# Two more weight slices loaded in column halves on two DMA queues, beside ScalarE's first table load

## The chip, the cores and the metric

One core of a Trainium2 chip. The metric is the device time of one execution in microseconds (us), of the slowest (here the only) core. In a profile, PE is TensorE's matmul stream, PEld its weight loads, DVE VectorE, ACT ScalarE, POOL GpSimd, SP SyncE; SPq and ACTq are the queues on which SyncE and ScalarE issue DMA loads. The "table load" is ACT_TABLE_LOAD, which in the trace stands on ScalarE just before its first activation (1.28 us, from 1.18 us on, in the kernel before).

## The reference

```python
def _fwd_reference(x, w1, w2):                 # x (1, 2048, 640), w1 (640, 1536), w2 (1536, 640), bf16
    h = jnp.einsum("bsd,df->bsf", x, w1)
    h = jax.nn.silu(h)
    return jnp.einsum("bsf,fd->bsd", h, w2)

def reference(x, w1, w2, grad_out):
    out, vjp = jax.vjp(_fwd_reference, x, w1, w2)
    return (out, *vjp(grad_out))               # out, and the gradients of x, w1, w2
```

## The kernel before

The change lies in the first 10 us. The kernel's first stage computes h for the first 512 rows of x. w1 lies in SBUF (the core's own memory, to which the loads go) as five row slices of 128 rows (k = 0 to 4, 384 KB each). The stage takes them in turn: for each slice twelve matmuls of 128x256, each pair of them accumulating into one of six tiles of PSUM (the memory to which matmuls write). So slice k has to be complete before its last matmuls, and slice k+1 is wanted 12 matmuls later.

```python
        def load_w1(k, cols=slice(0, F), eng=nc.sync):
            return eng.dma_start(out=w1_nat[:, k, cols], in_=w1_v[:, k, cols])

        early += [load_x(nc.sync, 0), load_x(nc.scalar, 1)]
        early += [load_w1(0, slice(0, F // 2)), load_w1(0, slice(F // 2, F), nc.scalar)]
        early += [load_w1(k) for k in range(1, 3)]
        for k in range(3, DT):
            load_w1(k)
        nc.sync.dma_start_transpose(out=xT_next[:, :, HC:SC], in_=x2[HC:SC, :])
        start_before_entry_wait(nc, {i.ins.name for i in early})   # moved ahead of the program's entry barrier
        nc.scalar.activation(warm_a[:], warm[:, 0:1], ACT.Silu)    # brings the first table load
        nc.sync.dma_start(out=w2_nat[:], in_=w2_v[:])
        goT_next = load_goT(0)
        # ... w2T and w1T by DMA transpose ...

        def h_first(xT, aT, ghT):
            pe_x(xT)                     # PE transposes of the two early x tiles
            # ...
            for dt_ in range(DT):        # slice by slice
                for pair in range(NPAIR):
                    h_pair_mm(hs[0][pair], pair, dt_, xT, halves[0])   # two matmuls
            # ... then the second 256 rows of x, with all slices present ...
```

The program's framework orders the instructions of each engine itself and gives each DMA one of eight completion semaphores. A DMA that takes over a semaphore waits until the DMA that had it before has landed: in the trace of this kernel the first eight loads have eight different semaphores, and the ninth DMA, the transpose of x's second half, is issued at 3.09, when the second x tile, whose semaphore it takes over, has landed (3.08).

## Time and profile before

| | before |
|---|---|
| time, median of 3 runs before the prediction | 320.84 us (320.25 to 321.2) |
| span of the profiled run | 318.8 us |
| PE busy | 313.6 us, 98% |
| first h stage: PE's idle time put down to w1 loads | 0.22 + 0.65 us |

Two lines of the profile's page, kernel before: the busy table (busy us, share of the span, count of instructions) and the chain of work that ended last, by engine.

```profile
PE 313.6 (98%) x1516; PEld 150.5 (47%) x1544; DVE 102.8 (32%) x182; ACT 76.8 (24%) x139; POOL 0.7 (0%) x6
...
PE 96%; DMA 2%; issue 1%; SPq 0%; DVE 0%; DVEq 0%
```

TensorE bounds the kernel. A change of loads can gain only what PE idles for them.

From the timeline of the first 20 us, kernel before (a selection of its lines): start in us, length in us, engine, source line, operation, output<-inputs, count, and in brackets how long the engine was idle and what ended that. w1's tile and tensor show as `w_nat` and `in_w_dram`.

```profile
0.09 0.39 SPq L183 DMA_DIRECT2D x_nat<-in_x_dram  x1
0.21 0.38 ACTq L183 DMA_DIRECT2D x_nat<-in_x_dram  x1
0.54 2.31 SPq L186 DMA_DIRECT2D w_nat<-in_w_dram  x5
0.61 0.45 ACTq L186 DMA_DIRECT2D w_nat<-in_w_dram  x1
1.18 1.28 ACT L195 ACT_TABLE_LOAD   x1 [1.18 <-ACTq L483]
3.09 3.79 SPq L193 DMA_TRANSPOSE xT<-in_x_dram  x1
3.85 1.72 PE L246 MATMUL hp<-xT,w_nat 128*128 128x256 bf16 x12
5.79 1.48 PE L246 MATMUL hp<-xT,w_nat 128*128 128x256 bf16 x12 [0.22 <-DMA w_nat<-in_w_dram]
7.92 10.65 PE L246 MATMUL hp<-xT,w_nat 128*128 128x256 bf16 x96 [0.65 <-DMA w_nat<-in_w_dram]
```

PE takes slice 0 at 3.85, waits a little for slice 1 (5.79), more for slice 2 (7.92), and never again. The chain of waits of the same stretch says the same from the other side: the longest wait was slice 2's load, issued at 1.47.

```profile
0.99 0.43 SPq L186
1.47 6.41 DMA w_nat<-in_w_dram
7.92 10.65 PE hp L246 x96
```

Each of these loads reports 16 times in the trace, and I take one report to be that of one of the core's 16 DMA engines: the semaphore records give the moment of each. I read them for each early load (this table is my own reading of the trace, in us from the span's start; "complete" is the sixteenth report):

```
kernel before          queue  issued  first of 16  complete
x tile 0               SP      0.09      2.12         2.60
x tile 1               ACT     0.21      2.53         3.08
slice 0, first half    SP      0.54      3.21         3.60
slice 0, second half   ACT     0.61      3.70         4.12
slice 1                SP      0.99      4.75         5.74
slice 2                SP      1.47      5.79         7.88
slice 3                SP      2.04      6.80         8.87
slice 4                SP      2.42      9.75         9.83
x transpose            SP      3.09     11.02        11.12
```

Slice 2 begins to report at 5.79, but its slowest engine needs 2.1 us longer. It is for that lag that PE stands idle for 0.65 us.

### The profile page before, as it was taken

How to read it: one execution, taken by the hardware profiler on the slowest of the kernel's cores; microseconds unless marked ns; L12 is line 12 of the kernel's file. 1: busy time of each engine (PE TensorE's matmuls, PEld its weight loads, DVE VectorE, ACT ScalarE, POOL GpSimd, SP SyncE). 2: the span in 40 equal slices, each digit the busy share in tenths (PEclk: the TensorE clock that was granted, in tenths of full speed). 3: DMA queues.
4: the chain of work that ended last, by engine and by line, in shares of the span. 5: the costliest groups of instructions: out<-in, count | busy, mean ns of one | idle time of the engine just before them, and what ended most of it. 6: DMA issues, size and time to landing. Idle time of an engine off the chain costs nothing.

```text
span 318.8 us, 3632 instructions
## 1 busy us (share of the span) xinstructions
PE 313.6 (98%) x1516; PEld 150.5 (47%) x1544; DVE 102.8 (32%) x182; ACT 76.8 (24%) x139; POOL 0.7 (0%) x6
## 2 busy tenths in 40 slices
PE   8999999999999999999999999999999999999997
PEld 6854444444444444444444444444444444444444
DVE  1495641477410087710147741000000100001001
ACT  2691000545201354411054520110100001001010
POOL 0000000000000000000000000000000000000000
DMA  8999999999989986492635079909999999997111
GB/s 280 293 181 192 221 249 260 349 252 280 292 214 343 230 155 176 169 310 76 168 110 141 0 256 267 221 20 297 211 245 254 204 251 326 236 313 217 65 35 49
DMA packets 147233, 67.02 MB, mean 210 GB/s; under 512 B 113937, under 2 KB 146705, under 8 KB 147217
## 3 DMA queue, kind: packets, MB, share of 16 engines
q1 hardware_dynamic: 146928, 66.43, 83.3%
q10 hardware_dynamic: 288, 0.36, 0.3%
q8 instruction: 12, 0.20, 0.2%
q14 instruction: 5, 0.03, 0.0%
HBM read 9.18 MB, written 28.97 MB: 120 GB/s over the span
## 4 chain that ended last, share of the span: by engine, by line
PE 96%; DMA 2%; issue 1%; SPq 0%; DVE 0%; DVEq 0%
PE hp L315 32%; PE hp L299 16%; PE hp L404 16%; PE hp L455 15%; PE hp L217 12%; PE hp L246 3%; DMA w_nat<-in_w_dram 2%; PE hp L435 1%; SPq L186 0%; SPq L183 0%; DVE g L446 0%; DVEq L446 0%; SPq L483 0%
## 5 line engine op out<-in xcount | busy, mean ns | idle before, releaser
L299 PE MATMUL hp<-goT,w2T 128*128 128x512 bf16 x239 | 56.8, 379 | 0.1
L315 PE MATMUL hp<-ghT,w1T 128*128 128x512 bf16 x235 | 52.2, 379 | 0.3
L315 PE MATMUL hp<-aT,w_nat 128*128 128x512 bf16 x234 | 52.1, 379 | 0.3
L404 PE MATMUL hp<-a_blk,go_nat 128*128 128x512 bf16 x235 | 51.7, 379 | 0.3
L455 PE MATMUL hp<-gh_blk,x_nat 128*128 128x512 bf16 x219 | 48.2, 379 | 0.3
L217 PE MATMUL hp<-xT,w_nat 128*128 128x512 bf16 x174 | 43.4, 379 | 0.3
L323 ACT ACTIVATE oT<-hp 128x512 bf16<-128x512 f32 x24 | 14.5, 604 | 106.8 <-PE hp L315 106.8
L299 PEld LDWEIGHTS <-w2T 128*128 128x128 bf16 x240 | 23.5, 98 | 28.3
L404 PEld LDWEIGHTS <-go_nat 128*128 128x128 bf16 x240 | 23.5, 98 | 28.3
L315 PEld LDWEIGHTS <-w1T 128*128 128x128 bf16 x240 | 23.4, 98 | 28.4
L315 PEld LDWEIGHTS <-w_nat 128*128 128x128 bf16 x240 | 23.5, 98 | 28.1
L306 DVE SCALAR_TENSOR_TENSOR ghT<-ghT,hp 128x512 bf16<-128x512 bf16 x48 | 32.5, 683 | 7.3 <-PE hp L299 7.3
L455 PEld LDWEIGHTS <-x_nat 128*128 128x128 bf16 x224 | 21.9, 98 | 26.4
L325 DVE CAST oT<-hp 128x512 bf16<-128x512 f32 x16 | 11.1, 691 | 72.2 <-PE hp L315 67.7
L226 ACT ACTIVATE aT<-hp 128x512 bf16<-128x512 f32 x36 | 21.5, 597 | 30.4 <-PE hp L217 30.4
L217 PEld LDWEIGHTS <-w_nat 128*128 128x128 bf16 x180 | 17.6, 98 | 21.2
L233 DVE SCALAR_TENSOR_TENSOR ghT<-aT,v 128x512 bf16<-128x512 bf16 x36 | 24.7, 686 | 0.2
L232 DVE TENSOR_SCALAR v<-t 128x512 bf16<-128x512 f32 x36 | 15.4, 427 | 26.7 <-ACT t L230 26.7
L230 ACT ACTIVATE t<-hp 128x512 f32<-128x512 f32 x36 | 21.3, 591 | 0.0
L466 DVE CAST g<-hp 128x512 bf16<-128x512 f32 x7 | 4.8, 692 | 47.0 <-PE hp L455 27.0
L414 DVE CAST g2T<-hp 128x512 bf16<-128x512 f32 x7 | 4.8, 692 | 46.1 <-PE hp L404 46.1
L412 ACT ACTIVATE g2T<-hp 128x512 bf16<-128x512 f32 x8 | 4.8, 597 | 47.0 <-PE hp L404 47.0
(28 smaller groups left out, 76.4 us busy)
## 6 DMA issues: line engine op xcount, KB each, us to landing
aT_scr<-aT SPq DMA_DIRECT2D x4, 1536.0 KB, 6.3
ghT_scr<-ghT SPq DMA_DIRECT2D x4, 1536.0 KB, 8.2
out_dram<-o_sb SPq DMA_DIRECT2D x8, 640.0 KB, 3.3
oT_scr<-oT SPq DMA_DIRECT2D x4, 640.0 KB, 3.6
go_nat<-in_grad_out_dram SPq DMA_DIRECT2D x4, 640.0 KB, 8.1
gxT_scr<-oT SPq DMA_DIRECT2D x4, 640.0 KB, 4.8
w_nat<-in_w_dram SPq DMA_DIRECT2D x1, 1920.0 KB, 11.0
x_nat<-in_x_dram SPq DMA_DIRECT2D x3, 640.0 KB, 7.4
```

What stands on the lines that cost most here:

```text
L217: nc.tensor.matmul(hp[:], lhsT=w1_nat[:, dt_, ft * P:(ft + 1) * P], rhs=xT[:, dt_, :], start=(dt_ == 0), stop=(dt_ == DT - 1),)
L226: nc.scalar.activation(aT[:, ft, :], hp[:], ACT.Silu)
L230: nc.scalar.activation(t[:], hp[:], ACT.Tanh, scale=0.5)
L232: nc.vector.tensor_scalar(out=v[:], in0=t[:], scalar1=-0.5, scalar2=0.5, op0=ALU.mult, op1=ALU.add)
L233: nc.vector.scalar_tensor_tensor(out=ghT[:, ft, :], in0=aT[:, ft, :], scalar=1.0, in1=v[:], op0=ALU.subtract, op1=ALU.mult)
L299: nc.tensor.matmul(gp[:], lhsT=w2T[:, dt_, ft * P:(ft + 1) * P], rhs=goT[:, dt_, :], start=(dt_ == 0), stop=(dt_ == DT - 1),)
L306: nc.vector.scalar_tensor_tensor(out=ghT[:, ft, :], in0=ghT[:, ft, :], scalar=1.0, in1=gp[:], op0=ALU.add, op1=ALU.mult)
L315: nc.tensor.matmul(op_[:], lhsT=w_all[:, ft, dt_ * P:(dt_ + 1) * P], rhs=rhs_all[:, ft, :], start=(ft == 0), stop=(ft == FT - 1),)
L323: nc.scalar.activation(oT[:, dt_, :], op_[:], ACT.Copy)
L325: nc.vector.tensor_copy(out=oT[:, dt_, :], in_=op_[:])
L404: nc.tensor.matmul(gp[:], lhsT=go_nat[:, st, dt_ * P:(dt_ + 1) * P], rhs=a_blk[:, st, :], start=(st == 0), stop=(st == ST - 1),)
L455: nc.tensor.matmul(gp[:], lhsT=x_nat[:, st, dt_ * P:(dt_ + 1) * P], rhs=gh_blk[:, st, :], start=(st == 0), stop=(st == ST - 1),)
```

## The change

The intent: slices 1 and 2 come in as slice 0 does, in two column halves of 192 KB on the two queues, so that both queues carry them; and ScalarE need not finish its table load before it issues its halves.

```diff
+    NSPLIT = 3
@@
-        early += [load_w1(0, slice(0, F // 2)), load_w1(0, slice(F // 2, F), nc.scalar)]
-        early += [load_w1(k) for k in range(1, 3)]
-        for k in range(3, DT):
+        for k in range(NSPLIT):
+            early += [load_w1(k, slice(0, F // 2)), load_w1(k, slice(F // 2, F), nc.scalar)]
+            if k == 0:
+                nc.scalar.activation(warm_a[:], warm[:, 0:1], ACT.Silu)
+        for k in range(NSPLIT, DT):
             load_w1(k)
         nc.sync.dma_start_transpose(out=xT_next[:, :, HC:SC], in_=x2[HC:SC, :])
         start_before_entry_wait(nc, {i.ins.name for i in early})
-        nc.scalar.activation(warm_a[:], warm[:, 0:1], ACT.Silu)
```

## The prediction

> **What bounds the kernel.** TensorE. The page's busy table has PE at 98% of the 318.8 us span (313.6 us), at granted clock 1.00, and the chain of waits is 96% PE. PE is idle for about 5 us. The windows table and the timeline put only 0.87 us of that where this change acts: the first h stage, which takes w1's row slices k = 0..4 in turn, 12 matmuls each. The PE timeline shows 12 matmuls from 3.85 us, an idle of 0.22 us ended by the w1 DMA (slice 1, restart at 5.79), 12 more, an idle of 0.65 us ended by the w1 DMA (slice 2, restart at 7.92), then no wait until 18.6. The chain's 2% "DMA w_nat" (1.47 to 7.88 us) is slice 2's flight. So the change's ceiling is about 0.9 us, 0.3% of the time.
>
> **What it moves.** Bytes stay the same. Two 384 KB loads on SyncE become four of 192 KB, two of them on ScalarE. The slices' packets shrink from 3072 to 1536 bytes: in the trace's packet records 121 ns against 65 ns, so 130 ns for the same bytes, 7% slower while the engines are full. From 2 to 8 us the DMA share is already 0.9 to 1.2 and 290 to 380 GB/s; with both queues active (2 to 4 us) it was 330 to 353, with one (4 to 8 us) 343. [...] Issue (0.43 us each) is not what is late: slice 2 was issued at 1.47 and landed 6.4 us later. By average rate slice 2 should be in at about 6.1 us; it is late since one of 16 engines lags. With two rings the lag may fall on fewer bytes: that is the hoped gain.
>
> **Side effects in the instruction order.** The ninth DMA reuses the first one's completion semaphore, so ScalarE's half of slice 2 waits for the first x tile (landed about 2.6 us) and is issued at about 2.6 to 3.0 instead of straight away. Its half of slice 1 should be issued at about 1.1 to 1.6, while the table load (1.28 us) runs. On SyncE slice 4 now waits for the second x tile (3.1 us; before issued at about 2.4), and the transpose of x's second half waits for the first half of slice 0 (about 3.6; before 3.09), about 0.5 us later. That transpose landed at 11.1 us and is needed at 11.9, minus the gain. Slice 3 has, by the packet records, about 0.3 us of slack. So part of the gain returns as waits for slice 3, slice 4 or the transpose. Later some SyncE stores swap with a transpose, where PE waits for no DMA: no effect.
>
> **Sum.** Slice 1 gap: -0.2 us. Slice 2 gap: -0.3 (of 0.65). Given back at slice 3 or the transpose: +0.1. Total about -0.4 us: 320.4 us, range 319.7 to 321.2, as three runs of the kernel before spread over 0.95 us. Faster by over 2%: 0.5%; within 2%: 99%; slower: 0.5%.
>
> **What would show it.** PE's second group starts at about 5.6, the third at 7.2 to 7.7; the sum of PE's waits for w1 falls from 0.9 to about 0.4 us; the last matmul of the first h stage ends about 0.4 us before 18.57; ScalarE's issues as timed above; the rest unchanged.
>
> **What would make it wrong.** ScalarE issues nothing until its table load and activation are done (2.7 us), so slice 2's second half lands later than before; the transpose turning critical; smaller packets slowing slices 3 and 4.

## The result, and the profile after

The changed kernel took 321.59 us (median of 6 runs, 320.93 to 321.85); the kernel before, in the same rounds and the earlier ones, 320.54 us (6 runs, 320.02 to 321.2). The ratio is 1.0027, with a 95% interval of 1.0009 to 1.0044. (Ratios here are the mean time of one kernel's runs over that of the other's of the same rounds, so not quite the ratio of the medians.) It is a small loss, inside the 2% that count as "same", but outside the predicted range of 319.7 to 321.2, and on the wrong side.

The page's two lines, changed kernel (span 320.1 us):

```profile
PE 314.8 (98%) x1544; PEld 150.2 (47%) x1544; DVE 102.6 (32%) x182; ACT 76.8 (24%) x139; POOL 0.7 (0%) x6
...
PE 96%; DMA 3%; issue 0%; DVE 0%; DVEq 0%; ACTq 0%
```

From the timeline of the first 20 us, changed kernel (a selection of its lines):

```profile
0.09 0.39 SPq L184 DMA_DIRECT2D x_nat<-in_x_dram  x1
0.21 0.38 ACTq L184 DMA_DIRECT2D x_nat<-in_x_dram  x1
0.54 2.39 SPq L187 DMA_DIRECT2D w_nat<-in_w_dram  x5
0.62 0.45 ACTq L187 DMA_DIRECT2D w_nat<-in_w_dram  x1
1.11 1.28 ACT L193 ACT_TABLE_LOAD   x1 [1.11 <-PEq L485]
1.17 0.39 ACTq L187 DMA_DIRECT2D w_nat<-in_w_dram  x1
2.97 0.34 ACTq L187 DMA_DIRECT2D w_nat<-in_w_dram  x1
...
3.83 1.47 PE L248 MATMUL hp<-xT,w_nat 128*128 128x256 bf16 x12
4.25 2.58 SPq L196 DMA_TRANSPOSE xT<-in_x_dram  x1
6.48 2.42 PE L248 MATMUL hp<-xT,w_nat 128*128 128x256 bf16 x18 [1.17 <-DMA w_nat<-in_w_dram]
9.91 10.00 PE L248 MATMUL hp<-xT,w_nat 128*128 128x256 bf16 x90 [1.02 <-DMA w_nat<-in_w_dram]
```

ScalarE issues its half of slice 1 at 1.17, while the table load runs (1.11 to 2.39): that part works as intended. Its half of slice 2 goes out only at 2.97. PE now waits until 6.48 for slice 1, takes 18 matmuls, and stands again until 9.91: those 18 are slice 1 and the first half of slice 2, and what is missing is slice 2's second half. The chain names it and what held its issue:

```profile
0.21 2.73 DMA x_nat<-in_x_dram
2.97 6.90 DMA w_nat<-in_w_dram
9.91 10.00 PE hp L248 x90
```

The load issued at 2.97 had to wait for the second x tile (0.21 to 2.94), because it took over that tile's completion semaphore. Then it was 6.9 us under way. The reports of the 16 engines, as above:

```
changed kernel         queue  issued  first of 16  complete
x tile 0               SP      0.09      2.08         2.59
x tile 1               ACT     0.21      2.50         2.95
slice 0, first half    SP      0.54      3.09         3.49
slice 0, second half   ACT     0.62      3.60         4.23
slice 1, first half    SP      0.99      4.08         6.43
slice 1, second half   ACT     1.17      4.70         7.36
slice 2, first half    SP      1.47      5.21         7.54
slice 3                SP      2.04      6.39         8.39
slice 4                SP      2.60      7.42         9.64
slice 2, second half   ACT     2.97      9.75         9.87
x transpose            SP      4.25     10.94        11.21
```

Two things stand out. First reports come in the order of issue, whichever queue a load is on. And the half that PE wants third-last of all is served last: slices 3 and 4, 768 KB that nobody wants yet, were issued before it. (Its sixteen reports came as one block, from 9.75 on; the 4-byte packets that carry them were sent from 7.54 to 9.53, so by the packets too it came after slice 4, whose first report was at 7.42, about 0.35 us after its packet.)

After this stage nothing differs. The last matmul of the stage starts at 18.30 before and 19.64 after; from there to the end of the span it is 300.5 us in both (318.8 - 18.30, 320.1 - 19.64).

### The profile page after: what moved, and what is told of

Read it like the earlier page. It is cut to its first block, busy times and chain, and to the rows that moved or that the text cites. A ratio compares the mean times of both kernels' runs of the same rounds, so it can differ in the third digit from the quotient of the medians.

```text
span 320.1 us, 3662 instructions
## 1 busy us (share of the span) xinstructions
PE 314.8 (98%) x1544; PEld 150.2 (47%) x1544; DVE 102.6 (32%) x182; ACT 76.8 (24%) x139; POOL 0.7 (0%) x6
## 4 chain that ended last, share of the span: by engine, by line
PE 96%; DMA 3%; issue 0%; DVE 0%; DVEq 0%; ACTq 0%
PE hp L317 32%; PE hp L301 16%; PE hp L406 16%; PE hp L457 15%; PE hp L219 12%; PE hp L248 3%; DMA w_nat<-in_w_dram 2%; PE hp L437 1%; DMA x_nat<-in_x_dram 1%; DVE g L448 0%; DVEq L448 0%; ACTq L485 0%
## 5 line engine op out<-in xcount | busy, mean ns | idle before, releaser
L248 PE MATMUL hp<-xT,w_nat 128*128 128x256 bf16 x120 | 13.8, 273 | 2.4 <-DMA w_nat<-in_w_dram 2.2
```

Of the source, the lines that this page charges most:

```text
L248: nc.tensor.matmul(hp[:, q, :], lhsT=w1_nat[:, dt_, ft * P:(ft + 1) * P], rhs=xT[:, dt_, cols], start=(dt_ == 0 and q == qs[0]), stop=(dt_ ...
```

## The experiments

My theory after reading the two traces was **issue order**: the two queues feed one line, loads are served in the order in which they are issued, and the late half of slice 2 stands behind slices 3 and 4. The rivals were **lateness** (an issue at 3 us is too late in itself, or ScalarE's queue holds a load back), **two rings** (the halves on the second queue lose their turns at the DMA engines to SyncE's loads), **packet size** (1536-byte packets in place of 3072), and **the table load's place**. All runs were correct; each was timed in 5 rounds against the kernel before on the same chip (three chips in all). There were eleven.

"PE waits" below is the sum of the gaps between the starts of the stage's 120 matmuls beyond a matmul's own pace, read from the trace; it counts a little more than the page's idle time, and not the wait before the first matmul (0.8 us in `dep_2b`, whose slice 0 was late).

| run | slice 1 complete | slice 2 complete | PE waits | slow matmuls | ratio (95% interval) |
|---|---|---|---|---|---|
| kernel before | 5.74 | 7.88 | 1.20 | 2 | 1 |
| changed kernel | 7.36 | 9.87 | 2.78 | 0 | 1.0027 (1.0009 to 1.0044) |
| after_again | 5.78 | 9.47 | 1.53 | 5 | 1.0028 (1.0005 to 1.0050) |
| late_sp | 7.74 | 10.27 | 3.16 | 1 | 1.0026 (1.0010 to 1.0042) |
| k2_act | 7.29 | 8.34 | 1.62 | 2 | 1.0057 (1.0029 to 1.0084) |
| split2 | 7.09 | 7.26 | 0.89 | 0 | 1.0006 (0.9993 to 1.0019) |
| tl_last | 6.61 | 7.21 | 0 | 12 | 0.9991 (0.9979 to 1.0003) |
| dep_2b | 6.08 | 6.88 | 0 | 22 | 0.9993 (0.9969 to 1.0017) |
| after_hold34 | 5.89 | 6.74 | 0.52 | 3 | 0.9992 (0.9974 to 1.0010) |
| tl_only | 6.87 | 7.81 | 0.57 | 9 | 1.0005 (0.9978 to 1.0032) |
| hold34 | 6.48 | 7.39 | 1.17 | 21 | 1.0006 (0.9981 to 1.0031) |
| halves_sp | 5.92 | 6.96 | 0 | 1 | 0.9985 (0.9973 to 0.9997) |
| halves_again | 5.82 | 6.80 | 0.39 | 5 | 0.9968 (0.9943 to 0.9993) |

("Slow matmuls" are explained at the end of this section. The one of `late_sp` falls where the clock was full, so it is a short stall rather than a slow matmul. The columns from a trace are one execution each, the ratio comes from 5 or 6 runs of the kernel against 11 of the kernel before; the changed kernel's first ratio has 6 and 6.)

### tl_last: the late half issued early

```diff
         for k in range(NSPLIT):
             early += [load_w1(k, slice(0, F // 2)), load_w1(k, slice(F // 2, F), nc.scalar)]
-            if k == 0:
-                nc.scalar.activation(warm_a[:], warm[:, 0:1], ACT.Silu)
@@
         start_before_entry_wait(nc, {i.ins.name for i in early})
+        nc.scalar.activation(warm_a[:], warm[:, 0:1], ACT.Silu)
```

> The changed kernel with the table load moved behind ScalarE's loads, as in the kernel before. By the instruction order ScalarE's half of slice 2 then has no wait and is issued at about 1.6 us instead of 2.97; all else is as changed. Late-issue theory (the ninth DMA's semaphore wait is what costs): slice 2 has landed by about 7.9 us, PE's waits for w1 fall from 2.2 to at most 0.9 us, time 320.3 to 320.6, no slower than before. Two-rings theory (the halves on the second queue lose their turn to later slices on the first): ScalarE's halves still land last, slice 2 after 8.5 us, PE waits about 2 us, time 321.2 to 321.8. If packets of ScalarE's slice 2 again begin only when its slice 1 has finished on the slowest DMA engine, the queue itself holds them.

Time 320.06 us (median of 6), ratio 0.9991. From the timeline of this run:

```profile
0.62 1.42 ACTq L187 DMA_DIRECT2D w_nat<-in_w_dram  x3
2.15 1.28 ACT L196 ACT_TABLE_LOAD   x1 [2.15 <-ACTq L484]
3.93 14.56 PE L247 MATMUL hp<-xT,w_nat 128*128 128x256 bf16 x120
```

ScalarE issues its three halves back to back; PE runs all 120 matmuls without a wait. Slice 2 is complete at 7.21, ScalarE's half of it reports first at 5.74. With the half issued at 1.58 the loss is gone, so neither the two queues nor the smaller packets as such cost it. Nor did ScalarE's queue hold a load here until its earlier one was complete: the packets of this half began at 5.07, and ScalarE's half of slice 1 was complete only at 6.61. The run does not yet say whether the half was late in itself or late in the order, since the same edit also moved slices 3 and 4 back: they now take over the x tiles' semaphores and are issued at 3.23 and 3.60.

### split2, k2_act, halves_sp: parts of the change, and one queue

`split2` sets NSPLIT to 2, so that slice 2 is whole on SyncE again. `k2_act` and `halves_sp` start from the kernel before:

```diff
# k2_act
-        early += [load_w1(k) for k in range(1, 3)]
+        early += [load_w1(1), load_w1(2, eng=nc.scalar)]
# halves_sp
-        early += [load_w1(k) for k in range(1, 3)]
+        for k in range(1, 3):
+            early += [load_w1(k, slice(0, F // 2)), load_w1(k, slice(F // 2, F))]
```

> The changed kernel with only slices 0 and 1 in halves on two queues; slice 2 is whole on SyncE again, and ScalarE's half of slice 1 is issued beside the table load at 1.17 us with no wait. Late-issue theory: nothing is late, time 320.2 to 320.6. Two-rings theory: ScalarE's half of slice 1 lands at about 6.5 to 7.4 us, later than whole slice 1 did before (5.7), and PE waits over 1 us in sum, time 320.7 to 321.4.

> Kernel before with whole slice 2 moved to ScalarE's queue behind its half of slice 0 (issued at about 1.1 us, no wait, 3072-byte packets). Two-rings theory: slices 1 and 2 now share the engines, slice 1 lands later than 5.7 us (6 to 6.5) and slice 2 about 7 to 8 us beside slices 3 and 4; PE waits 0.9 to 1.5 us, time 320.5 to 321.0. Late-issue theory: slice 2 is early, PE waits 0.5 or less, time 320.0 to 320.4.

> Kernel before with slices 1 and 2 in two column halves, but all four halves on SyncE's queue: packet size and DMA count change, the order of the queue does not. Packet-size theory: slices 1 and 2 land later and the time is 321.2 or more, as in the changed kernel. Two-rings and late-issue theories: as the kernel before, slice 2 at about 7.9 to 8.1 us, PE waits 0.9 to 1.1 us, time 320.4 to 320.8.

`split2` took 320.60 us, ratio 1.0006: with only slice 1 in halves there is no loss that these runs can show. In its trace slice 1 is complete at 7.09, as the two-rings theory said, but slice 2 follows at 7.26 and PE's waits sum to 0.89.

`halves_sp` took 319.95 us, ratio 0.9985: the packet-size theory falls, for the same 1536-byte packets on one queue were not slower but faster than the kernel before, and faster than any theory had expected. Its timeline has PE's stage all in one piece:

```profile
4.16 13.46 PE L247 MATMUL hp<-xT,w_nat 128*128 128x256 bf16 x120
```

`k2_act` took 321.59 us, ratio 1.0057, the worst of all; two of its six runs, at 323.64 and 324.05, pull the mean up. Every theory had this one better. Its loads report first in the order of issue too (slice 1 on SyncE, issued 0.99, at 4.66; slice 2 on ScalarE, issued 1.10, at 5.92), but with both whole slices issued 0.11 us apart, slice 1's slowest engine came in only at 7.29 instead of 5.74. PE in the first 12 us (the view cuts the last group there):

```profile
4.10 1.78 PE L246 MATMUL hp<-xT,w_nat 128*128 128x256 bf16 x12 [0.25 <-DMA w_nat<-in_w_dram]
7.34 4.87 PE L246 MATMUL hp<-xT,w_nat 128*128 128x256 bf16 x43 [1.46 <-DMA w_nat<-in_w_dram]
```

That trace explains about 0.7 us (the stage's last matmul starts at 19.03 against 18.30), not the two slow runs, one of which had a mean granted clock of 0.995; without these two the mean is still 1.003 of the kernel before. So here the loads were in the right order and the loss was as large as the changed kernel's, and no run tells why. There may be something in the two-rings theory for whole slices that are issued together; the runs below show that it is not needed for the changed kernel's loss.

### after_hold34 and late_sp: lateness against order, and the queue against order

`after_hold34` keeps the late half late (it waits for a VectorE copy that needs the second x tile) and moves only slices 3 and 4 behind it, by the same means. Order edges for the scheduler, which add no wait, keep SyncE's later loads in program order.

```diff
+            if k == 2:
+                nc.vector.tensor_copy(out=w1_nat[:, k, F // 2:F // 2 + 1], in_=x_nat[:, 1, 0:1])
             early += [load_w1(k, slice(0, F // 2)), load_w1(k, slice(F // 2, F), nc.scalar)]
@@
+        # three times, so that the loads below are issued a little later still
+        nc.vector.tensor_copy(out=w1_nat[:, 3:DT, 0:1], in_=x_nat[:, 1:2, 0:2].rearrange("p a b -> p b a"))
         for k in range(NSPLIT, DT):
-            load_w1(k)
+            in_turn(load_w1(k))       # and so on for SyncE's later loads
```

> The changed kernel with ScalarE's half of slice 2 still issued late (it waits for the second x tile, about 3.0 us), but slices 3 and 4 issued only after it (their SyncE loads wait for a tiny VectorE copy that needs the second x tile; about 3.3 and 3.7 us instead of 2.04 and 2.60). Issue-order theory (both queues feed one line, loads are served in the order of issue, whichever the queue): the late half now goes ahead of slices 3 and 4, its first landing is at about 5.8 to 6 us and its last at about 7 to 7.5 instead of 9.87; PE waits for w1 at most 0.9 us; time 320.0 to 320.6. Lateness theory (an issue at 3 us is too late in itself, or ScalarE's queue holds a load until its earlier one is complete): lands at 9 us or later, PE waits about 2 us, time 321.2 to 321.8.

`late_sp` keeps the order of the changed kernel but takes slice 2 off ScalarE's queue:

```diff
         for k in range(NSPLIT):
-            early += [load_w1(k, slice(0, F // 2)), load_w1(k, slice(F // 2, F), nc.scalar)]
+            early += [load_w1(k, slice(0, F // 2))]
+            if k < 2:
+                early += [load_w1(k, slice(F // 2, F), nc.scalar)]
             if k == 0:
                 nc.scalar.activation(warm_a[:], warm[:, 0:1], ACT.Silu)
         for k in range(NSPLIT, DT):
             load_w1(k)
+        load_w1(2, slice(F // 2, F))
```

> The changed kernel with the second half of slice 2 on SyncE instead of ScalarE, issued behind slices 3 and 4. No load of slice 2 is on ScalarE's queue. Issue-order theory: it lands last whatever its queue, at 9 us or later, PE waits 2 us or more, time 321.2 to 322.0, as the changed kernel or a little more. ScalarE-queue theory (the second queue is served worse): better than the changed kernel, 320.8 or less.

These two decide it. From the timeline of `after_hold34`, then from that of `late_sp`, of the first 12 us (the last group of each is cut there; in `late_sp` six loads of SyncE stand in one line, the late half being the last of them):

```profile
3.36 0.33 ACTq L199 DMA_DIRECT2D w_nat<-in_w_dram  x1
4.06 4.45 PE L265 MATMUL hp<-xT,w_nat 128*128 128x256 bf16 x36
8.87 3.34 PE L265 MATMUL hp<-xT,w_nat 128*128 128x256 bf16 x29 [0.35 <-DMA w_nat<-in_w_dram]
```

```profile
0.54 3.13 SPq L187 DMA_DIRECT2D w_nat<-in_w_dram  x6
1.17 0.39 ACTq L187 DMA_DIRECT2D w_nat<-in_w_dram  x1
7.02 2.25 PE L251 MATMUL hp<-xT,w_nat 128*128 128x256 bf16 x18 [1.28 <-DMA w_nat<-in_w_dram]
10.31 1.92 PE L251 MATMUL hp<-xT,w_nat 128*128 128x256 bf16 x16 [1.04 <-DMA w_nat<-in_w_dram]
```

In `after_hold34` the half was issued at 3.36, even later than in the changed kernel, on the same queue and in the same size; yet it reported first at 5.63 and was complete at 6.74, because slices 3 and 4 were issued at 3.84 and 4.21. Its packets began at about 4.9, 1.5 us after the issue; in the changed kernel they began at 7.01, 4.0 us after it. PE ran slices 0 to 2 (36 matmuls) in one piece; its one wait is for slice 3. The time was 320.28 us, ratio 0.9992. In `late_sp` the half was on SyncE, issued at 3.25 behind slices 3 and 4; it was complete at 10.27, PE stopped after the same 18 matmuls, and the time was 321.43 us, ratio 1.0026, the same loss as the change. Lateness and the queue are out; the place in the order of issue is in. (The intervals of the two ratios just touch, at 1.0010, so it is above all the landings in the traces that carry this.)

### dep_2b and tl_only: the table load's place

`dep_2b` is the change as it was meant: the table load stays where the change put it, and an order edge (no wait) makes the scheduler place slices 3 and 4 after ScalarE's half of slice 2, which so becomes the eighth DMA and needs no semaphore that is in use. `tl_only` is the other part of the change by itself:

```diff
# tl_only, from the kernel before
         early += [load_w1(0, slice(0, F // 2)), load_w1(0, slice(F // 2, F), nc.scalar)]
+        early.append(nc.scalar.activation(warm_a[:], warm[:, 0:1], ACT.Silu))
         early += [load_w1(k) for k in range(1, 3)]
@@
-        nc.scalar.activation(warm_a[:], warm[:, 0:1], ACT.Silu)
# dep_2b, from the changed kernel
         for k in range(NSPLIT, DT):
-            load_w1(k)
+            in_turn(load_w1(k))       # follows early[-1], ScalarE's half of slice 2, in the schedule
```

> The changed kernel as it was meant: table load where the change puts it, SyncE's later loads made to follow in program order, so that ScalarE's half of slice 2 is the eighth DMA, has no wait, and is issued at about 1.6 us beside the table load; slices 3 and 4 then wait for the x tiles (about 3.1 us). Issue-order and late-issue theories: as the run with the table load last (0.9991 of before): slice 2 landed by about 7.2 us, time 320.0 to 320.6. If the table load's place is what costs: about 321.5, as the changed kernel.

> The kernel before with only the table load moved in front of the entry wait, behind ScalarE's half of slice 0; no further halves, no DMA added, so no semaphore wait moves. All theories that blame the loads: as before, ratio 0.999 to 1.001, slices landing as before. If the table load's place itself costs: ratio above 1.001.

`dep_2b` issued the half at 1.58, beside the table load, and had slice 2 complete at 6.88; 320.47 us, ratio 0.9993. `tl_only` took 320.78 us, ratio 1.0005, with slices 1 and 2 complete at 6.87 and 7.81. Neither shows a cost of the table load's place. It hurt only by what it did to the schedule: in the changed kernel slice 3 is among the eight loads with a semaphore of their own, and ScalarE's half of slice 2 is not; in `tl_last` and `dep_2b` it is the other way round.

### after_again and halves_again: repeats on one chip

> The changed kernel once more, beside the two below on one chip, for a second trace of it. Issue-order theory: ScalarE's half of slice 2 is again issued near 3 us, after slices 3 and 4, its first landing comes after theirs, slice 2 is complete at 9 us or later, ratio to before 1.001 to 1.0045. If the first trace was an accident of one lagging engine, the half lands ahead of slice 4 this time and the ratio is within 1.001 of 1.

> The fastest kernel so far (halves of slices 1 and 2 all on SyncE, 0.9985 of before) once more, to see whether its lead over the kernel before stands and whether its landings repeat: slice 2 complete at about 7 us, no wait of PE for slices 1 and 2, ratio 0.997 to 1.000. Were the first result chance, the ratio would be 1.000 to 1.001 and slice 2 at about 7.9.

The changed kernel again took 321.44 us, ratio 1.0028. From the timeline of its second trace, the first 12 us (the last group is cut there):

```profile
3.27 0.33 ACTq L187 DMA_DIRECT2D w_nat<-in_w_dram  x1
4.07 4.08 PE L248 MATMUL hp<-xT,w_nat 128*128 128x256 bf16 x30
9.51 2.69 PE L248 MATMUL hp<-xT,w_nat 128*128 128x256 bf16 x23 [1.37 <-DMA w_nat<-in_w_dram]
```

Here slice 1 was in time (5.78): the wait for it in the first trace belonged to that execution's lagging engine. What repeats is the wait in the middle of slice 2: 30 matmuls, then nothing until its second half is complete at 9.47. `halves_sp` again was the fastest: 319.87 us, ratio 0.9968. So a version that beats both kernels is the one with halves, but all of them on SyncE's queue, in the order in which PE wants them. Its lead over the kernel before is 0.15% to 0.3%.

### hold34: why are halves on one queue faster?

In `halves_sp` slices 3 and 4 also go out later (3.17 and 3.54), since two more DMAs come before them and they take over the x tiles' semaphores. `hold34` gives the kernel before that delay alone, with the VectorE copy of above in front of slices 3 and 4.

> The kernel before (slices 1 and 2 whole, on SyncE) with slices 3 and 4 issued only when the second x tile has landed (about 3.2 us instead of 2.04 and 2.42). Asks why halves on SyncE alone were faster than before (0.9985): there slices 3 and 4 also waited. Holding theory (loads queued further back slow the lagging engines of the slices in front): the spread of the 16 landings of slice 2 falls from 2.1 to 1.5 us or less, slice 2 lands at about 7.2 instead of 7.88, time 319.8 to 320.2. Packet theory (smaller packets are what shortened the spread): as before, slice 2 at about 7.9, time 320.4 to 320.7.

It took 320.64 us, ratio 1.0006 (0.9981 to 1.0031): not settled. The landings moved nearly as the holding theory said (spread of slice 2's reports 1.5 us, complete at 7.39), but the time lies where the packet theory had it, and the interval holds both. Over the other traces the picture is mixed: the reports of slice 2's last load are spread over 1.0 to 1.5 us in all six traces where slice 3 was held to 2.7 us or later; where it was issued by 2.05 us they are spread over 2.0 to 2.4 us in the kernel before, `tl_only` and `k2_act`, but over 1.0 us in `split2`. One trace for each kernel is too little to call that shown.

### Slow matmuls: why traces and times differ by a microsecond

`tl_last` has no wait in the stage and yet ends it at nearly the same moment as the kernel before. Busy time by stretch, `tl_last` and then `halves_sp` (stretch and its length in us, then busy us and counts of PE, PEld, DVE, ACT and POOL, the granted clock, DMA share and GB/s):

```profile
4.00:6.50 2.50, 2.50 (x13) 1.71 (x13) 0.42 (x1) 0.39 (x1) 0.00 (x0) 1.00 1.00 342
6.50:9.00 2.50, 2.50 (x24) 2.21 (x23) 0.00 (x0) 0.00 (x0) 0.00 (x0) 1.00 1.10 267
```

```profile
4.00:6.50 2.50, 2.38 (x21) 2.03 (x21) 0.42 (x1) 0.44 (x1) 0.00 (x0) 1.00 0.99 342
6.50:9.00 2.50, 2.50 (x25) 2.23 (x24) 0.00 (x0) 0.00 (x0) 0.00 (x0) 1.00 1.10 297
```

PE is busy all the time in both, but for the first 0.12 us of `halves_sp`, yet in its first stretch `tl_last` gets through 13 matmuls where `halves_sp` gets through 21. Start to start, its matmuls take 0.21 us there and 0.109 us later. So a slow matmul of 256 columns takes about twice as long as the later ones (0.21 / 0.109 = 1.9). The traces show a switch with it: eight traces have both slow matmuls and a record of the granted clock, and in each of them the first record of full clock begins within 0.25 us of the start of the last slow matmul (at 6.63 in `tl_last`, 4.58 in `halves_sp`, 9.46 in `dep_2b`). In the ten traces that have such records full clock lasts 317.44, 314.03 or 310.61 us: steps of 3.41. The slow matmuls number from 0 (changed kernel, first trace) to 22 (`dep_2b`), about 0.1 us each, up to 2.3 us in one execution; between the two traces of one kernel they differ too (0 and 5 for the changed kernel, 1 and 5 in `halves_sp` and `halves_again`). What sets the moment of the switch is not shown. The slow matmuls are not what the change lost: its first trace was at full clock from 3.39 us on, before the stage began, and still ended the stage 1.3 us later. This is why a single span decides nothing here, and why the medians with their intervals and the landings carry the argument.

## Why the prediction was wrong

- *What bounds the kernel, and the ceiling of 0.9 us*: right. Only the first h stage changed; the 300.5 us behind it are the same.
- *ScalarE issues beside the table load*: right, at 1.17 during a load from 1.11 to 2.39. The load takes 1.28 us, as in the kernel before and in `tl_last`.
- *Its half of slice 2 is issued at about 2.6 to 3.0, since it takes over a semaphore*: right in time (2.97). The tiles were swapped: it waited for the second x tile (2.95) and slice 4 for the first (issued at 2.60, predicted 3.1); the x transpose went out at 4.25 instead of 3.6, and this cost nothing (complete at 11.21 against 11.12).
- *The step that failed*: "With two rings the lag may fall on fewer bytes: that is the hoped gain", and with it the term "Slice 2 gap: -0.3". I had seen that the half would be issued late, and gave the lateness no cost, because I took ScalarE's queue for a ring of its own whose loads get their turns at once beside whatever SyncE's queue holds, which no trace had shown. The term came out with the other sign: PE's wait for slice 2 was 1.02 and 1.37 us in the two traces, where 0.65 was to shrink by 0.3. Nor did the lag shrink with the bytes: from first to last report the three halves that were issued in time took 2.3 to 2.7 us in the first trace and 1.2 to 1.9 in the second; whole slices 1 and 2 had taken 1.0 and 2.1. The runs agree with one line in the order of issue. In all 13 traces the first reports of all early loads come in the order of issue across both queues, about 0.55 us apart for 192 KB in a full line. The half was behind slices 3 and 4, four times 192 KB, 2.2 us; its first report would otherwise be due at about 5.7 (`tl_last`, `dep_2b`), so at about 7.9 (its first report packet was sent at 7.54, and reports follow these packets by about 0.35 us, though this one was withheld until 9.75); with the 2 us or so from the first engine to the last that slices 3 and 4 took in this trace this makes 9.9, and 9.87 was measured. `after_hold34` takes those 2.2 us away and leaves the rest, `late_sp` leaves them and takes the queue away.
- *PE's waits fall from 0.9 to about 0.4 us*: wrong. By the page's measure they rose to 2.2 us (1.17 + 1.02), of which 1.02 is for slice 2; the 1.17 for slice 1 did not come again in the second trace.
- *What would make it wrong*: I named "slice 2's second half lands later than before", but for the reason that ScalarE would issue nothing during its table load. The harm was the one named; the reason was the order.
- *Smaller packets, 7% slower*: visible as packet times (median 65 ns for 1536 bytes, 121 ns for 3072, in the kernel before and in the changed one), but no loss (`halves_sp` is faster than the kernel before, ratio 0.9985).

What stays open: whether halves on one queue win by their smaller pieces or by holding slices 3 and 4 back; why `k2_act` is slow, its two slowest runs above all; whether a second queue by itself makes slice 1 later (complete at 5.8 to 7.7 where half of it came on ScalarE's queue, at 5.7 to 6.9 where nothing of slices 1 and 2 did, too few traces to tell); and why the DMA engines report up to 2 us apart.

## What to carry to other kernels

In these runs loads on two issuing engines were not two lanes. So ask in which order the loads are issued over both engines, and issue them in the order in which they are wanted. When a change adds a DMA or moves an instruction of an issuing engine, look at the built order for a load that takes over a completion semaphore still in use; a load issued 1.4 us later here (2.97 against 1.58 in `tl_last`) landed more than 2 us later (slice 2 complete at 9.87 against 7.21), since the queue next door went ahead in the meantime. And look for loads that nobody wants yet but that are issued early: letting slices 3 and 4 wait cost PE at most 0.35 us here (`after_hold34`, a wait for slice 3), and letting them go first made the half that PE wanted more than 2 us later (9.87 against 6.74).

## What else these traces show

- In the changed kernel the load issued on ScalarE at 2.97 sent its first packet at 7.0 us, after SyncE's loads issued at 2.04 and 2.60 had begun (171 of their 256 packets had started), and in 13 of 13 traces first reports follow the order of issue over both queues. Whether the late load's work had reached the DMA engines before that, the traces do not show.
- The best version has the halves of slices 1 and 2 on one queue (0.9985 and 0.9968); the two-queue versions without a misplaced load have 0.9991 to 1.0006. A second queue can go with a loss: `k2_act`, also without a misplaced load, has 1.0057.
- The load issued just before the x transpose reports as a block: in the changed kernel the late half's sixteen reports lie between 9.75 and 9.87 us, though the 4-byte packets that carry them were sent between 7.54 and 9.53. In all 13 traces at least fifteen of the sixteen reports of that load lie within about 0.1 us. That the transpose causes it is not tested. It cost nothing here, since the last engine was late anyway (its packet at 9.53, the last report at 9.87).
- The records of the granted clock agreed with the spacing of the matmuls (0.21 and 0.109 us for 256 columns) in eight of eight traces, but three traces have none, and none begins before the switch: so the windows view above reads 1.00 in a stretch where the matmuls run at half pace (`tl_last`, 4.00 to 6.50, first record at 6.63). The spacing of the matmuls, or the start of the first record, has to be looked at.
